# A recurrent attention kernel: the largest matrix product in row pairs of 64 rows, one pool of eight PSUM banks, and a searched scheduling bias

## The chip, the cores and the metric

The kernel runs on one core of a Trainium2 chip. The metric is the device time of one execution in microseconds (us), the median of several. A ratio is the mean time of one kernel's fast runs over that of the kernel before in the same rounds, so it is not quite the ratio of the medians that are quoted. Engines: PE is the matrix engine (PEld its weight loads), DVE is VectorE, ACT is ScalarE, POOL is GpSimd. PSUM is the memory of the tiles b, into which PE writes its sums (`b<-hT,Mw` in the profile). The granted clock is the mean share of its full clock that PE was allowed.

## The reference

Four residual layers in a row: attention, gated feed-forward, attention, feed-forward, each on the layer norm of x (2048 tokens of width 448). The attention layer has 16 heads of 256 and runs through 64 segments of 32 tokens, one after the other. Eight rows of memory go from each segment to the next, which makes the whole a recurrence:

```python
for s in range(n_seg):
    h = jnp.concatenate([mem, xs], axis=1)              # 8 + 32 rows
    q, k, v = h @ Wq, h @ Wk, h @ Wv                    # per head
    p = softmax(where(mask, q @ k.T * scale, -1e9))
    o = (p @ v) @ Wo
    mem = o[:, :M, :]
    outs.append(o[:, M:, :])
```

## The kernel before

The kernel multiplies the weights together once: M = Wq x Wk per head, N = Wv x Wo per head. A step is one segment of both attention layers (68 steps; the second layer runs four segments behind the first, and 60 steps have work for both layers, hence 80 columns). Its largest product is T = M x h: 56 blocks of 128 outputs (16 heads x 448 = 56 x 128), contraction 448, which the kernel pads to four tiles of 128 rows:

```python
def t_unit(self, t, c, u0, m):                 # m blocks into one PSUM bank
    R = S.tile("R", 1)
    def mms():
        b = R.b()
        return [MM(b[:, j*n:j*n + n], S.M[:, kt, 16*c + u0 + j, :],      # weights 128 x 128
                   S.hT[:, pp, s, kt, l0:l1, :].rearrange(...),         # moving 128 x n, n = 80
                   start=(kt == 0), stop=(kt == 3))
                for j in range(m) for kt in range(4)]
    S.mm(mms, 4 * m * S.pitch(n), rd, R.res() + dst)
    # ... then copies out of PSUM into TTm and TTs
```

That is 56 x 4 = 224 matmuls a step, each with a weight load of its own. A step goes on with the memory's scores (TTm x hT), a softmax, the product with h (PTm x hK), with N (Nw x UTm), the choice of the new memory rows (selm, and seln for a second layout), and the same for the segment (TTs x hT, PTs x hK, Nw x big); every second step also runs a feed-forward (xBT x big, hB x big).

The kernel divides PSUM into eight banks. A pool "R" hands out five of them; bank 4 is for the sums of Nw x big and of the feed-forward, banks 6 and 7 for the memory's chain:

```python
POOLS = {"R": [0, 1, 2, 3, 5]}
self.bO, self.bC = bank[4], bank[6:8]
# m_t writes b0 = bC[0]; m_nat, the seln product, writes the same b0
```

A scheduler orders all operations at build time with a small model of the engines. It keeps for each engine the time at which it comes free, counts a matmul of n columns as `max(25, n/2.4 + 2.6)` ns and a change of tile shape as 95 ns, and takes the ready operation with the longest path behind it:

```python
lim = max(f, t0) + (60.0 if e == "pe" else 40.0)
t, o = max((x for x in lst if x[0] <= lim), key=lambda x: (x[1].prio, -x[0]))
...
c = o.cost[e]
if e == "pe" and o.mode != mode:
    c += 95.0
    mode = o.mode
```

## Time and profile before

| | before |
|---|---|
| median, 3 runs | 1780.73 us (1775.98 to 1781.08) |
| span of the profiled execution | 1780.3 us |
| matmuls, each with a weight load | 30612 |
| granted clock of the matrix engine | 0.989 |

From the page of the kernel before, the busy times of the engines and, of its queues, the one that brings instructions (packets, MB, share of 16 engines):

```profile
PE 1700.7 (96%) x30612; PEld 1226.7 (69%) x30612; DVE 1073.2 (60%) x3058; ACT 720.6 (40%) x2031; POOL 91.0 (5%) x156
...
q8 instruction: 241, 3.95, 0.9%
```

PE is busy 96% of the span, so it is the bottleneck. Its busy time also counts the tails of pipelined matmuls (one of T takes 202 ns in the mean in the profile, and the next starts 36 ns after it), so a finer measure is wanted: the distance from the start of one matmul to the start of the next in the trace. Its median in this trace is 25 ns at 16 and at 40 columns, 36 ns at 80, 56 ns at 128 and 189 ns at 448. n/2.4 + 2.6 ns, with a floor of 25 ns, fits all of them; I call it the undisturbed *pitch*. The sum of the pitches of all matmuls is the *stream*, with concurrent tiles counted once, and all the rest of PE's time is *gaps*. The stream is thus a count of the work and not a measurement: it is the same for every kernel with the same matmuls, and time lost to a lower clock falls under gaps. Before: stream 1583 us, gaps 187 us.

The groups of instructions by form of the kernel before (count; busy us and mean ns; idle before them and what ended it):

```profile
L127 PE MATMUL b<-hT,Mw 128*128 128x80 bf16 x13440 | 496.5, 202 | 3.6 <-DVE hT L685 3.6
...
L127 PE MATMUL b<-hi,seln 128*128 128x448 bf16 x67 | 24.2, 360 | 14.9 <-ACT hT L684 14.9
```

The first line is T. The other is the seln product: it waits for ACT's copy into hT, since both use bank 6. Who made PE wait, longest total first (us in total, times, longest):

```profile
PE b L127 <- ACT hT L684: 14.9, 32, 0.5
PE b L127 <- DVE xn L721: 14.0, 21, 5.5
PE b L127 <- DVE XA L1008: 7.1, 14, 0.5
PE b L127 <- issue: 6.1, 6, 3.3
```

And one pass of T in the timeline (start, duration, both in us):

```profile
907.84 8.19 PE L127 MATMUL b<-hT,Mw 128*128 128x80 bf16 x224
```

That is 224 matmuls in 8.19 us including the tail of the last.

### The profile page before, as it was taken

What the parts mean: (1) busy time and instruction counts of PE and PEld (TensorE: products, weight loads), DVE (VectorE), ACT (ScalarE), POOL (GpSimd) and SP (SyncE); (2) the same over time, 40 slices, a digit from 0 to 9 for tenths busy, and PEclk for the clock granted to TensorE, in tenths of its full rate; (3) what the DMA queues carried; (4) which work ended last, traced back from release to release, by engine and by line L of the source; (5) the groups of instructions that cost most, each with busy time, mean ns of one, the idle gap of its engine ahead of it and who ended that gap; (6) DMA issues with size and microseconds to landing.
All of it is one profiled execution on the core that took longest, in us unless ns stands there. A gap on an engine that the chain in (4) does not pass through costs nothing.

```text
span 1780.3 us, 67770 instructions
## 1 busy us (share of the span) xinstructions
PE 1700.7 (96%) x30612; PEld 1226.7 (69%) x30612; DVE 1073.2 (60%) x3058; ACT 720.6 (40%) x2031; POOL 91.0 (5%) x156
## 2 busy tenths in 40 slices
PE   6899999999999999999999999999999999999997
PEld 2566766777677667767766776776677677667765
DVE  7647565565656556565655656565665656566554
ACT  5433433444443334444333444334344433434432
POOL 3000000000000000000000000000000000000000
PEclk9999999999999999999999999999999999999999
DMA  9700000000000000000000000000000000000000
GB/s 227 219 4 4 4 5 5 4 5 5 5 4 5 5 4 5 5 5 4 5 5 4 5 5 5 4 5 4 4 5 6 5 4 5 3 3 4 4 4 5
DMA packets 55760, 27.52 MB, mean 15 GB/s; under 512 B 44584, under 2 KB 54576, under 8 KB 55472
## 3 DMA queue, kind: packets, MB, share of 16 engines
q1 hardware_dynamic: 55120, 22.94, 5.3%
q8 instruction: 241, 3.95, 0.9%
q14 instruction: 47, 0.39, 0.1%
q10 hardware_dynamic: 352, 0.24, 0.1%
HBM read 10.33 MB, written 1.84 MB: 7 GB/s over the span
## 4 chain that ended last, share of the span: by engine, by line
PE 75%; DVE 6%; ACT 2%; issue 1%; DVEq 0%
PE b L127 75%; ACT big L684 1%; DVE big L685 1%; DVE stat L714 1%; DVE TTs L685 1%; DVE xn L721 1%; ACT hT L684 1%; DVE ys L1015 1%; DVE XA L1008 1%; DVE XB L968 0%; DVE Es L843 0%; DVE stat L842 0%; DVE TTm L685 0%; DVE hT L685 0%; DVE part L957 0%
## 5 line engine op out<-in xcount | busy, mean ns | idle before, releaser
L127 PEld LDWEIGHTS b<-hT,Mw 128*128 128x128 bf16 x15232 | 539.8, 100 | 25.3 <-DVE hT L685 11.2
L127 PE MATMUL b<-hT,Mw 128*128 128x80 bf16 (+1 forms) x15232 | 546.0, 200 | 5.0 <-DVE hT L685 4.6
L127 PE MATMUL b<-Nw,big 128*128 128x448 bf16 (+1 forms) x1936 | 394.9, 358 | 8.2 <-DVE big L685 5.6
L685 DVE CAST TTs<-b 128x320 bf16<-128x320 f32 (+5 forms) x574 | 261.3, 455 | 78.6 <-PE b L127 78.3
L127 PEld LDWEIGHTS b<-Nw,big 128*128 128x128 bf16 (+1 forms) x1936 | 163.7, 100 | 157.1 <-issue 21.5
L127 PE MATMUL b<-xBT,big 128*128 128x128 bf16 (+1 forms) x3808 | 219.6, 217 | 0.7 <-ACT xBT L684 0.7
L685 DVE CAST TTm<-b 128x80 bf16<-128x80 f32 (+5 forms) x580 | 134.7, 232 | 129.5 <-PE b L127 98.0
L127 PEld LDWEIGHTS b<-xBT,big 128*128 128x128 bf16 x3808 | 204.7, 98 | 2.4 <-ACT xBT L684 0.9
L127 PE MATMUL b<-Nw,UTm 128*32 128x448 bf16 x3752 | 192.0, 356 | 0.6 <-ACT UTm L684 0.6
L685 DVE CAST big<-b 128x512 bf16<-128x512 f32 (+1 forms) x190 | 121.3, 659 | 103.9 <-PE b L127 102.8
L684 ACT ACTIVATE big<-b 128x512 bf16<-128x512 f32 (+1 forms) x322 | 153.7, 525 | 48.2 <-PE b L127 45.0
L127 PEld LDWEIGHTS b<-Nw,UTm 128*32 128x32 bf16 x3752 | 95.2, 97 | 88.9 <-issue 18.7
L685 POOL COPY hK<-xn 32x448 bf16<-32x448 bf16 x136 | 75.6, 556 | 1521.6 <-DVE xn L721 1470.4
L684 ACT ACTIVATE TTs<-b 64x256 bf16<-64x256 f32 (+5 forms) x310 | 127.6, 412 | 29.6 <-PE b L127 22.4
L995 ACT ACTIVATE gT<-b 128x256 bf16<-128x256 f32 x226 | 86.4, 382 | 128.8 <-PE b L127 124.1
L684 ACT ACTIVATE TTm<-b 64x64 bf16<-64x64 f32 (+4 forms) x304 | 69.4, 228 | 159.4 <-PE b L127 152.5
L996 DVE TENSOR_TENSOR hB<-gT,b 128x256 bf16<-128x256 bf16 x226 | 93.6, 415 | 64.8 <-ACT gT L995 54.0
L896 ACT ACTIVATE hi<-b 128x448 bf16<-128x448 f32 x67 | 36.5, 544 | 193.7 <-PE b L127 193.5
L897 DVE TENSOR_TENSOR lo<-b,hi 128x448 bf16<-128x448 f32 x67 | 41.4, 619 | 121.2 <-ACT hi L896 121.2
L127 PE MATMUL b<-big,hB 128*128 128x448 bf16 (+1 forms) x476 | 107.3, 355 | 0.0
L684 ACT ACTIVATE hK<-b 8x448 bf16<-8x448 f32 x94 | 50.4, 536 | 122.5 <-PE b L127 121.0
L127 PE MATMUL b<-PTs,hK 40*128 40x512 bf16 (+1 forms) x640 | 86.4, 348 | 13.3 <-DVE XA L1008 7.1
(103 smaller groups left out, 1396.1 us busy)
## 6 DMA issues: line engine op xcount, KB each, us to landing
big<-in_A_Wo_dram SPq DMA_DIRECT2D x3, 896.0 KB, 5.8
out_dram<-ys SPq DMA_DIRECT2D x32, 56.0 KB, 1.9
big<-in_B_W_down_dram SPq DMA_DIRECT2D x1, 1568.0 KB, 6.8
XA<-in_A_x_dram SPq DMA_DIRECT2D x28, 56.0 KB, 2.0
big<-in_B_W_up_dram SPq DMA_DIRECT2D x1, 1344.0 KB, 8.1
big<-in_B_W_gate_dram SPq DMA_DIRECT2D x1, 1344.0 KB, 8.5
Nw<-in_A_Wo_dram SPq DMA_DIRECT2D x1, 896.0 KB, 6.4
XA<-in_A_x_dram ACTq DMA_DIRECT2D x4, 56.0 KB, 4.3
```

The source lines that it names most:

```text
L127: ins = E.matmul(out, lhsT=lhsT, rhs=rhs, **kw)
L684: return E.activation(out(), src(), ACT.Copy)
L685: return E.tensor_copy(out(), src())
L714: S.dve(lambda E: E.bn_stats(st[:, so:so + 6], x), D, rd, [(key, 0)])
L721: S.dve(lambda E, a=a, b=b, src=src: E.tensor_scalar(S.xn[:, i, a:b], src, st[:, so + 6:so + 7], st[:, so + 8:so + 9], op0=ALU.subtract, o ...
L896: S.act(lambda E: E.activation(S.hi[:, :], b[:, 0:D], ACT.Copy), D, S.ps(6), [("hi",)])
L897: S.dve(lambda E: E.tensor_tensor(S.lo[:, :], b[:, 0:D], S.hi[:, :], ALU.subtract), D, S.ps(6) + [("hi",)], [("lo",)])
L995: S.act(lambda E, k=k, R=R, n=n: E.activation(S.gT[:, k % 2, 0:n], R[0].b()[:, 0:n], ACT.Relu), n, R[0].res(), [("gT", k % 2)])
L996: S.dve(lambda E, k=k, R=R, n=n, fcs=fcs: E.tensor_tensor(S.hB[:, fcs[0]:fcs[-1] + 1, 0:w], S.gT[:, k % 2, 0:n].rearrange("p (a b) -> p a ...
L1008: S.dve(lambda E: E.tensor_tensor(S.XA[64:128, q % 4, :], S.bO[0:64, 0:D], S.XB[0:64, p % 2, :], ALU.add), D, S.ps(4, half=(0,)) + xb, [(" ...
L1015: S.dve(lambda E: E.tensor_tensor(S.ys[64:128, p % 2, :], S.bO[64:128, 0:D], S.XB[64:128, p % 2, :], ALU.add), D, S.ps(4, half=(1,)) + xb, ...
```

## The change

The intent is to take the padding out of T. A product with only 64 rows leaves the other 64 of 128 free, and two such products on different row halves can run at once: in the trace before, the two matmuls of a row pair of PTm x hK start 3 to 4 ns apart, and pairs of 128 columns follow each other after 56 ns, the pitch of a single 128-column matmul (the first pair after a change of tile shape takes 67 ns). T is cut into pieces of 64 rows (448 = 7 x 64), and two blocks A and B go side by side: first A on the upper half of the rows and B on the lower, then exchanged. A slot is the time of one matmul, or of two that run at once. A pair of blocks takes 14 matmuls in 7 slots; the 28 pairs of a step take 392 matmuls in 196 slots, where 224 slots were used before. In this kernel the two halves write to different banks, and the second half of a group waits for its first. All eight banks go into one pool, and each kind of work gets a bias on its priority, found by an offline search that minimises the span in the scheduler's own engine model. The core of the diff (the rest renames fixed banks to pool tiles):

```diff
+BIAS = {
+    "b_down": -20822.0, "b_layer": 11731.0, "ln_a": 5000.0, "ln_b": 8278.0, "m_nat": -8730.0, "m_t": 19893.0,
+    "p_t_mem": 13944.0, "s_mem": 20000.0, "s_seg": 38611.0, "seg_pt": 10000.0, "t_pass": 80290.0, "u_mem":
+    -2223.0, "u_seg": -245.0, "un": -6353.0, "un_mem": -500.0,
+}
...
-    POOLS = {"R": [0, 1, 2, 3, 5]}
+    POOLS = {"R": list(range(8))}
...
+        for o in self.ops:
+            o.prio += BIAS.get(o.cat, 0.0)
...
-        self.M = self.sb("Mw", [128, 4, NO, 128])
+        self.M = self.sb("Mw", [128, 3, NO, 128])
+        self.M3 = self.sb("M3", [128, NO // 2, 128])
...
+                    if not second:
+                        for kt in range(3):
+                            out.append(MM(a[:, v], S.M[top, kt, oa + j, :], mov(kt, top), start=(j == kt == 0), stop=False))
+                            out.append(MM(b[:, v], S.M[bot, kt, ob + j, :], mov(kt, bot), start=(j == kt == 0), stop=False))
+                        out.append(MM(a[:, v], S.M3[top, slot0 + j, :], mov(3, top), start=False, stop=False))
+                        out.append(MM(b[:, v], S.M3[bot, slot0 + j, :], mov(3, bot), start=False, stop=False))
+                    else:
+                        for kt in range(3):
+                            e = j == m - 1 and kt == 2
+                            out.append(MM(b[:, v], S.M[top, kt, ob + j, :], mov(kt, top), start=False, stop=e))
+                            out.append(MM(a[:, v], S.M[bot, kt, oa + j, :], mov(kt, bot), start=False, stop=e))
...
+            S.mm(mms, (3 if second else 4) * m * S.pitch(n), rd + rd2 if second else rd, ..., mode=1)
```

The last line tells the model that a pair costs one pitch: 4 or 3 slots a block pair, each 36 ns.

## The prediction

> **What bounds the kernel now.** The matrix engine. The page's first part has PE busy 1700.7 of 1780.3 us, VectorE 60%, ScalarE 40%; DMA is idle after two of 40 slices; PE is at 9 tenths nearly throughout, at full clock. I split PE time by the matmuls' start-to-start distances in the trace. They follow n/2.4 + 2.6 ns with a floor of 25 ns: 36 ns at 80 columns, 56 at 128, 189 at 448. With concurrent tiles counted once, these pitches sum to about 1583 us. The other 187 us are gaps: about 74 us in 721 changes of tile shape (95 to 125 ns each), 40 us of start-up, 70 us of steady waits. The largest: the seln matmul waiting for ScalarE's hT copy, as both use one fixed bank (18 us), PTs x hK waiting for VectorE (14 us), the first Nw x big waiting for the copy into big (12 us).

> **What changes.**
> 1. T (Mw x hT) was 224 matmuls per step, contraction padded from 448 to 512 rows: 8.05 us per step, 528 us in all. It becomes 392 matmuls of 64 rows, two at once on different row halves and banks: 196 slots. If a pair costs one pitch: 28 slots x 36 ns x 60 two-layer steps + 28 x 25 ns x 8 others = **-66 us**. Row pairs already in the trace (PTm x hK, 40x128) start 3 ns apart, and pairs follow each other after 56 ns, as one 128-column matmul would; the first pair after a shape change loses 11 ns, as a single full load does, so two loads run together. [...] Not shown: four instructions per 36 ns sustained for 7 us; the trace sustains two per 25 ns.
> 2. Shape changes: 697 instead of 721 by the order listing: -2 us.
> 3. Eight banks in one pool, no fixed banks: removes the 18 us wait and part of the others. I credit **-20 us** net, bias included.
> 4. Costs: T's copies still take VectorE and ScalarE about 9 us of work per step; the new order wants the segment scores (TTs x hT) about 1 us after T, when copies may still run (0.1 to 0.4 us per step). 32 more setup copies, at most 3 us. PE's wait for its own first half is covered by 0.5 us or more of another pair.

> **On the path.** PE is the bottleneck, so removed stream time counts fully while the recurrence (about 18.6 us in the timeline) stays under the step period (26 us, then about 25).

> **Prediction: 1692 us**, range 1655 to 1740. Chances: faster by over 2% 0.88, within 2% 0.07, slower 0.05.

> **What would show each step.** (1) T's stretch in the timeline 7.0 to 7.2 us for 392 matmuls, pairs 36 ns apart. (2) 95 to 125 ns before and after T. (3) No ScalarE hT wait before hi x seln; PE idle down from about 80 to about 60 us. (4) Idle before TTs x hT released by VectorE or ScalarE.

> **What would make it wrong.** If pairs are limited by instruction issue or loads (50 ns a pair), T takes 9.8 us and the kernel gets slower than before. If copies or banks stall the pairs inside T, gain shrinks towards 1740. If the search removes most steady waits, about 1660.

The sum: 1780 - 66 - 2 - 20 = 1692 us.

## The result

| | before | changed |
|---|---|---|
| median, 4 runs each | 1780.9 us | 1877.3 us (1876.34 to 1885.94) |
| ratio of fast runs | | 1.0552 (95%: 1.051 to 1.0594) |
| matmuls | 30612 | 42036 |
| changes of tile shape on PE | 721 | 697 |
| stream (pitches of all matmuls) | 1583 us | 1517 us |
| gaps | 187 us | 347 us |
| granted clock of the profiled execution | 0.989 | 0.974 |
| pass of T, first to last matmul start, median of 60 | 8.11 us | 9.41 us (shortest 8.68) |

The change is slower by 5.5%, where 5% faster was predicted. The stream is smaller by the 66 us that the prediction gave it; as it is counted with the same pitches, that is arithmetic. What the trace confirms is the pitch: one pair of T starts 36 ns after the other (median), as one 80-column matmul does. The gaps grew by 160 us. From the page of the changed kernel, the same two lines:

```profile
PE 1663.3 (89%) x42036; PEld 1185.6 (63%) x42036; DVE 974.5 (52%) x2797; ACT 805.8 (43%) x2459; POOL 88.0 (5%) x155
...
q8 instruction: 332, 5.44, 1.2%
```

PE is busy for less time, in a longer span; it idles more. The instruction queue brought 332 packets instead of 241. The same groups of instructions ("hT,M" is the new array M3, its number left out):

```profile
L131 PE MATMUL b<-hT,Mw 64*128 64x80 bf16 x20160 | 454.7, 198 | 105.5 <-issue 103.6 <-PE b L131 1.0 <-DVE hT L699 0.6
...
L131 PE MATMUL b<-hT,M 64*128 64x80 bf16 x3360 | 264.8, 198 | 18.0 <-issue 18.0
...
L131 PE MATMUL b<-hi,seln 128*128 128x448 bf16 x67 | 23.6, 352 | 0.0
```

The seln product waits for nothing now, as predicted. But the two groups of T stand 124 us idle, nearly all of it "issue": time in which the engine waited for nothing that the profile shows. Who made PE wait:

```profile
PE b L131 <- issue: 167.5, 161, 4.8
PE b L131 <- DVE xn L735: 23.0, 32, 6.2
...
PE b L131 <- PE b L131: 1.0, 1, 1.0
```

"PE b <- PE b" would be the wait for the first half: 1.0 us in all. So in this profile neither banks nor copies nor the first half hold T up. The timeline in one pass of T shows where the idle time lies:

```profile
906.44 0.20 PE L131 MATMUL b<-hT,M 64*128 64x80 bf16 x2
906.48 0.23 PE L131 MATMUL b<-hT,Mw 64*128 64x80 bf16 x3
907.63 0.24 PE L131 MATMUL b<-hT,Mw 64*128 64x80 bf16 x3 [0.92 <-issue]
907.68 0.24 PE L131 MATMUL b<-hT,M 64*128 64x80 bf16 x2
...
909.37 0.23 PE L131 MATMUL b<-hT,M 64*128 64x80 bf16 x2
909.40 0.70 PE L131 MATMUL b<-hT,Mw 64*128 64x80 bf16 x28
911.51 0.41 PE L131 MATMUL b<-hT,Mw 64*128 64x80 bf16 x8 [1.41 <-issue]
...
913.04 0.74 PE L131 MATMUL b<-Nw,big 128*128 128x448 bf16 x3
```

Between two stalls T runs at its full pace (64 pairs in 2.3 us, 36 ns a pair); the stalls fall at odd places, in the middle of a group. Counting instructions explains the places. In program order, a matmul is two instructions (load and product, 42036 of each in the trace), anything else one (871 here). The changed kernel has 84943 instructions for PE, 331.8 blocks of 256; the instruction queue brought 332 packets, each of 16384 bytes, 64 for each of 256 instructions. The kernel before has 61792, 241.4 blocks, and its queue brought 241 packets. In the trace 145 of the 146 stalls of over 0.15 us inside T begin at position 193 to 197 of a block of 256, together 183 us. The other stall is 0.5 us. The queue itself, in the DMA view of this pass cut into 40 slices of 0.26 us (GB/s, then packets, MB and share):

```profile
GB/s 0 0 0 0 0 0 0 62 0 0 0 0 0 0 0 0 0 0 0 0 0 62 0 0 0 0 0 0 0 0 0 0 0 0 0 0 0 62 0 0
...
q8 instruction: 3, 0.05, 2.2%
```

Three refills in the pass, one for each block that T uses up, near 904.9, 908.8 and 912.8 us. Over the whole trace a refill starts a median of 2.5 us before the stall that it ends (162 cases), and the next refill starts only after the engine has entered the new block: 1.2 us after the end of the stall in the median of the 146, 1.06 us at the soonest. Where two stalls end in successive blocks, 3.75 us lie between them (median of 94 cases, shortest 3.35). A block of T's row pairs is used up in 2.3 us. A block of the old T took 4.6 us (128 matmuls x 36 ns), longer than those 3.75 us, and it shows no such stalls (one in the whole trace).

One rival has to be set aside first: the granted clock fell from 0.989 to 0.974. The clock of both kernels in 40 slices of the span, in tenths of full speed, before and changed:

```profile
PEclk9999999999999999999999999999999999999999
PEclk9879999999999999999999999999999999999878
```

The lower clock lies at the start and the end. From 200 to 1700 us it is 1.00 in both traces, and 118 of the 146 stalls, 137 us, begin there. PE ran at half clock (128-column matmuls 107 ns apart instead of 56) for 98 us in all, against 40 us before; at most half of the other 58 us is lost by it, an estimate that leaves most of the 160 us to something else.

### The profile page after: what moved, and what is told of

Read it like the earlier page. It is cut to its first block, busy times and chain, and to the rows that moved or that the text cites. A ratio compares the mean times of both kernels' runs of the same rounds, so it can differ in the third digit from the quotient of the medians.

```text
span 1874.5 us, 91186 instructions
## 1 busy us (share of the span) xinstructions
PE 1663.3 (89%) x42036; PEld 1185.6 (63%) x42036; DVE 974.5 (52%) x2797; ACT 805.8 (43%) x2459; POOL 88.0 (5%) x155
## 5 line engine op out<-in xcount | busy, mean ns | idle before, releaser
L131 PE MATMUL b<-hT,Mw 64*128 64x80 bf16 (+1 forms) x22848 | 503.3, 196 | 134.2 <-issue 131.9
L131 PEld LDWEIGHTS b<-hT,Mw 64*128 64x128 bf16 x22848 | 479.2, 97 | 167.0 <-issue 149.8
L131 PE MATMUL b<-Nw,big 128*128 128x448 bf16 (+1 forms) x1936 | 412.4, 357 | 1.4 <-issue 1.4
L131 PE MATMUL b<-hT,M 64*128 64x80 bf16 (+1 forms) x3808 | 293.4, 196 | 24.7 <-issue 24.7
L699 DVE CAST TTm<-b 128x80 bf16<-128x80 f32 (+6 forms) x448 | 97.9, 226 | 388.0 <-PE b L131 387.1
L698 ACT ACTIVATE TTm<-b 128x80 bf16<-128x80 f32 (+6 forms) x504 | 106.5, 224 | 388.9 <-PE b L131 388.2
L131 PEld LDWEIGHTS b<-hT,M 64*128 64x128 bf16 x3808 | 202.9, 97 | 25.7 <-issue 25.7
L699 DVE CAST TTs<-b 128x320 bf16<-128x320 f32 (+5 forms) x476 | 200.6, 432 | 5.9 <-PE b L131 5.9
L698 ACT ACTIVATE TTs<-b 128x320 bf16<-128x320 f32 (+5 forms) x476 | 180.1, 396 | 6.6 <-PE b L131 6.6
L698 ACT ACTIVATE big<-b 128x512 bf16<-128x512 f32 x317 | 159.7, 566 | 5.4 <-PE b L131 3.8
```

Of the source, the lines that this page charges most:

```text
L131: ins = E.matmul(out, lhsT=lhsT, rhs=rhs, **kw)
L698: return E.activation(out(), src(), ACT.Copy)
L699: return E.tensor_copy(out(), src())
```

## The experiments

The table collects the accounting of all versions of the whole kernel, worked out from each trace as above, the granted clock of the profiled execution among it; "block end" is the sum of stalls over 0.15 us inside T at positions 192 to 198 of 256. Medians are of 4 runs, in each case beside runs of the kernel before on the same chip.

| run | T | banks, bias | median us | ratio | stream | gaps | shape changes | block end in T | granted clock |
|---|---|---|---|---|---|---|---|---|---|
| before | full | fixed, none | 1780.9 | 1 | 1583 | 187 | 721 | 0.5 | 0.989 |
| changed | pairs | pool, searched | 1877.3 | 1.055 | 1517 | 347 | 697 | 182.8 | 0.974 |
| e1_full | full | pool, same | 1903.2 | 1.069 | 1583 | 307 | 608 | 3.2 | 0.958 |
| e3_nobias | pairs | pool, none | 1956.4 | 1.100 | 1517 | 436 | 1167 | 76.0 | 0.937 |
| e5_hybrid | last 64 rows paired | pool, same | 1715.7 | 0.964 | 1517 | 186 | 940 | 7.0 | 0.991 |
| e7_pairs_only | pairs | fixed, none | 2115.1 | 1.187 | 1517 | 584 | 1324 | 21.3 | 0.953 |
| e8_full_nobias | full | pool, none | 1766.3 | 0.991 | 1583 | 172 | 677 | 1.9 | 0.990 |
| e9_hybrid_nobias | last 64 rows paired | pool, none | 1809.8 | 1.016 | 1517 | 281 | 1033 | 1.7 | 0.953 |
| e10_hybrid_re | last 64 rows paired | pool, searched again | 1685.2 | 0.947 | 1517 | 153 | 908 | 2.3 | 0.994 |
| e11_refill | pairs | pool, searched with a refill rule | 1824.6 | 1.022 | 1517 | 299 | 887 | 85.5 | 0.988 |

All of them gave correct results. In e1, e3, e7 and e9 the granted clock is lower through the whole span: their traces show PE at half clock for 163, 248, 200 and 172 us, in many short stretches, against 23 to 98 us in the others. In e9 one 80-column matmul starts 67 ns after the other there, and 36 ns elsewhere. In the stretches of e1 and e9 that were looked at, the half clock comes just after a wait of PE (3.0 us in e1, 1.4 us in e9); no run tests what starts it.

### e6_probe: the disputed cost by itself

Four runs of 1024 matmuls were added at the end of the kernel before, on PE alone:

```diff
+            for s, v in ends:              # ACT, DVE and POOL have finished
+                E.wait_ge(s, v)
+            def full(n, count):
+                for i in range(count):
+                    E.matmul(S.banks[0][:, 0:n], lhsT=S.M[:, i % 3, i % NO, :], rhs=mv[:, 0:n], start=True, stop=True)
+            def pairs(n, count):
+                for i in range(count // 2):
+                    for h, b in ((slice(0, 64), 1), (slice(64, 128), 2)):
+                        E.matmul(S.banks[b][:, 0:n], lhsT=S.M[h, i % 3, i % NO, :], rhs=mv[h, 0:n], start=True, stop=True)
+            full(80, 1024); pairs(80, 1024); full(16, 1024); pairs(192, 1024)
```

> The kernel before, with four runs of 1024 matmuls each (2048 instructions, eight blocks of 256) added at its end, on the matrix engine alone, with nothing to wait for and results unused: full array 80 columns, row pairs 80 columns, full array 16 columns, row pairs 192 columns. F: pairs of 80 columns take 27 to 31 us instead of 18.4 us, with a stall of over 1 us at most block ends; the 16 columns, at 25 ns a matmul 25.6 us if unlimited, take 27 to 31 us too though they are no pairs; full 80 columns take 36 to 38 us and pairs of 192 columns 42 to 44 us, with no stalls. D: pairs of 80 columns take 18 to 20 us, for there is no bank, copy or half to wait for. A theory that row pairs as such stall (banks or rows colliding): pairs of 192 columns stall too, and 16 full columns don't.

Measured, start of the first to start of the last: 36.65, 27.45, 29.43 and 44.57 us (one run; the clock at the pairs of 80 columns was 1.00). The timeline of the probe's stretch:

```profile
1779.87 36.85 PE L506 MATMUL b<-hT,Mw 128*128 128x80 bf16 x1024 [1.43 <-issue]
1816.66 3.36 PE L511 MATMUL b<-hT,Mw 64*128 64x80 bf16 x177
1821.01 2.47 PE L511 MATMUL b<-hT,Mw 64*128 64x80 bf16 x128 [0.99 <-issue]
1824.49 2.47 PE L511 MATMUL b<-hT,Mw 64*128 64x80 bf16 x128 [1.01 <-issue]
1827.96 2.47 PE L511 MATMUL b<-hT,Mw 64*128 64x80 bf16 x128 [1.01 <-issue]
...
1844.23 1.38 PE L506 MATMUL b<-hT,Mw 128*128 128x16 bf16 x49
1846.44 7.05 PE L506 MATMUL b<-hT,Mw 128*128 128x16 bf16 x256 [0.82 <-issue]
1853.66 3.58 PE L506 MATMUL b<-hT,Mw 128*128 128x16 bf16 x128 [0.16 <-issue]
...
1861.15 12.69 PE L506 MATMUL b<-hT,Mw 128*128 128x16 bf16 x463 [0.17 <-issue]
1873.77 44.81 PE L511 MATMUL b<-hT,Mw 64*128 64x192 bf16 x1024
```

With nothing to wait for, pairs of 80 columns stop after every 128 matmuls, that is every 256 instructions, for 1.0 to 1.6 us. Blocks last 3.46 to 4.02 us instead of the 2.3 us that the same pairs take without the stall. Only the first full block of pairs, which follows slow ones, passes in 2.3 us; the first stop comes 177 matmuls (354 instructions) after the pairs began. Pairs of 192 columns, whose blocks last 5.28 us, never stop. So row pairs as such run freely; it is the number of instructions in a time that is limited. That rules out theory D for these stalls. The full array with 16 columns is less clean: it also stopped at block ends, though it has no pairs, but for 0.16 us most times, and the mean granted clock was 0.57 in this stretch, and a matmul took 26.7 ns rather than 25. It agrees with F, but does not carry it. The total of the last run passed the expected 44 us by 0.6; the clock was 0.94 there.

### e5_hybrid: the same slots with fewer instructions

Only the odd 64 rows of the contraction need pairing. The other 384 rows are three full tiles:

```diff
-        part(g, R[g], False) ... part(g, R[g], True)      # 392 matmuls of 64 rows
+    PLAN = [("full", (0, 1)), ("rows", (0, 1, 2)), ("full", (2, 3)), ("rows", (3, 4, 5)), ("full", (4, 5))]
+        # full(g): kt = 0, 1, 2 of both units of pair g on the full array, 128 rows
+        for j in range(m):
+            for kt in range(3):
+                out.append(MM(T.b()[:, j*n:j*n + n], S.M[:, kt, 16*c + u0 + j, :], S.hT[:, pp, s, kt, l0:l1, :], ...))
+        # rows(gs): the last 64 rows, unit A on the upper half, unit B on the lower
+        for j in range(m):
+            out.append(MM(R[g][0].b()[:, v], S.M3[top, slot0 + j, :], mov(3, top), start=st, stop=e))
+            out.append(MM(R[g][1].b()[:, v], S.M3[bot, slot0 + j, :], mov(3, bot), start=st, stop=e))
```

That is 168 + 56 = 224 matmuls in 168 + 28 = 196 slots. The pool, the bias and the rest are the changed kernel's.

> The changed kernel with only the last 64 rows of T's contraction in row pairs (56 matmuls in 28 slots, in two bursts), the other 384 rows in 168 full matmuls: the same 196 slots as the change, with 448 instructions a step instead of 784, and four changes of tile shape a step inside T. F: a block of 256 instructions lasts about 4.0 us in T, longer than the 3.75 us refill, so stalls at block ends nearly vanish (under 0.3 us a step); T takes 7.3 to 7.9 us with its shape changes; time 1680 to 1740 us. D: banks are held as long as in the change or longer and copies start later, so the stalls inside T stay (over 1 us a step), time over 1780 us.

Measured: 1715.73 us, ratio 0.9638 (95%: 0.9621 to 0.9656), T in 7.71 us (median). The two lines of its page:

```profile
PE 1648.6 (96%) x30612; PEld 1173.3 (68%) x30612; DVE 998.0 (58%) x2909; ACT 778.5 (45%) x2347; POOL 87.7 (5%) x155
...
q8 instruction: 242, 3.96, 0.9%
```

The instructions are back at 242 packets, PE is busy 96% again, and the stalls at block ends inside T fell from 183 to 7 us, 0.1 us a step. T holds no fewer banks at once (six during a burst) and its copies are the same, so waits for banks or copies don't explain the 183 us either. The cost that the split brings is also in the table: 243 more changes of tile shape than the changed kernel. Inside T, where nothing else is waited for, one costs 98 ns (median of 272), about 24 us in all, an estimate from these two numbers. This version beats both kernels.

### e1_full, e3_nobias, e8_full_nobias, e9_hybrid_nobias: what the bias and the pool do

e1 puts the old T into the changed kernel (`t_pass` calls `t_unit` above for each unit; M has four tiles again); e3 sets `BIAS = {}`; e8 does both; e9 is e5 with `BIAS = {}`.

> The changed kernel with T put back on the full array (224 matmuls of 128 rows a step); eight banks in one pool and the bias kept. Theory F (the matrix engine's instruction stream is refilled in blocks of 256 instructions; a refill takes about 3.75 us when T's row pairs use one up in 2.3 us): the stalls at one fixed place in every block of 256 disappear, the steps' stream grows back by 66 us to about 1583 us, and the time is 1695 to 1755 us, with 5.6 us or less lost inside all T passes. Theory B (the searched bias made a worse order): still at or above 1800 us. Theory D (the pairs wait for banks, copies or their own first half): also fast, so this run does not tell F from D.

> The changed kernel with every bias set to nothing; row pairs and the pool of eight banks kept. F: T still stalls about twice a step for 1.1 us at the same place of each block of 256 instructions (100 us or more in all, unless other work happens to be placed inside T); time 1830 to 1930 us. B: time at or under 1780 us and the stalls inside T gone.

> The changed kernel with T on the full array and no bias: the kernel before with the pool of eight banks alone. It tells why the full array with the searched bias took 1903 us. If the bias, searched for another T, is what hurts there: 1740 to 1800 us. If the pool of eight banks hurts by itself: 1830 us or more. F expects no stalls at the block ends in either case.

> The version with only the last 64 rows paired, without the bias. F: no stalls at block ends; the time tells what the bias is worth to a T that does not stall. If the bias is worth about what it was between the two versions with full pairs (1956 against 1877 us, 79 us): 1760 to 1830 us.

e1 missed its time: 1903.2 us, not 1695 to 1755. Its stalls at block ends are gone as F said (3 us), but other waits came. Who made its PE wait:

```profile
PE b L131 <- DVE xn L735: 57.3, 33, 5.1
PE b L131 <- DVE Pm L830: 43.9, 16, 3.0
PE b L131 <- issue: 7.3, 4, 3.3
```

The new waits are for DVE's layer norm (xn) and the memory's softmax (Pm), not for instructions. e8 shows why: the same kernel without the bias takes 1766.28 us (ratio 0.9908, 95%: 0.9881 to 0.9936). So the bias, searched for the model's idea of row pairs, costs an old T 137 us (1903.2 - 1766.3; up to 63 us of it can be the clock, half of the 163 - 36 us more at half clock), and the pool of eight banks alone is worth 0.9%. e3 took 1956.38 us, above the 1830 to 1930 expected, with 76 us of stalls at block ends rather than 100 or more; I put that down to other work between T's parts (1167 changes of tile shape), which stretches the blocks. So here the bias helps by 79 us, although it packs T tightly and more than doubles the stalls (76 to 183 us). For the hybrid it helps by 94 us (1809.8 to 1715.7), within the 1760 to 1830 us that was expected of e9. Both gains go together with the clock, which is lower without the bias (0.937 against 0.974, and 0.953 against 0.991), so how much of them is a better order alone is not shown. Theory B falls as the cause of the loss: taking the bias away from the changed kernel makes it slower. But the bias is worth what it is worth only together with the T that it was searched for.

### e7_pairs_only: row pairs in the kernel before

The changed `t_pass`, `t_copies`, M3 and the wait for the first half were put into the kernel before, with its fixed banks and no bias.

> The kernel before with T in row pairs alone: fixed banks, pool of five, no bias. The order listing shows 1324 changes of tile shape against 721, because without the bias the scheduler puts other work between T's parts; at about 100 ns each that costs 60 us. F: stream -66 us, shape changes +60 us, and stalls at the same place in the blocks of 256 instructions, fewer than in the change because other work inside T stretches the blocks (0.5 to 2 per step, 40 to 140 us): 1810 to 1930 us. If the pool or the bias were the cause instead of the pairs, this one shows no such stalls and takes 1760 to 1790 us.

Measured: 2115.08 us, ratio 1.187, far outside the expected range. The stalls at block ends inside T are only 21 us; other stalls came in their place: 125 further gaps of 119 us inside T. Who made its PE wait:

```profile
PE b L131 <- DVE TTs L689: 133.3, 181, 1.2
PE b L131 <- DVE Es L893: 54.1, 28, 1.9
```

With five banks in the pool, T waits for DVE to copy TTs out. Here theory D's mechanism is real and I had not reckoned with it: T has four banks in work and two more being copied, which five banks can't serve, and without the bias the order is poor besides. The parts of the change can't be added up one by one.

### e10_hybrid_re: the bias searched again

The same search idea (random steps on the biases, keeping what shortens the scheduler's own span, 840 seconds) was run for the hybrid:

```diff
-BIAS = { ... the changed kernel's ... }
+BIAS = {"b_down": -22829, "b_layer": 26760, "ln_a": 86029, "ln_b": 75302, "m_nat": -12510, "m_t": 203841, "p_t_mem": 529037,
+        "s_mem": 23429, "s_seg": 17526, "seg_pt": -6015, "t_pass": 127155, "u_mem": -5686, "u_seg": -2501, "un": -14682, "un_mem": 210608}
```

> The version with only the last 64 rows paired, its bias searched again with the kernel's own engine model for this T (840 seconds of a random search; the same shape of T, 908 changes of tile shape instead of 940). If the model is sound wherever blocks of instructions last over 3.75 us: faster than the 1716 us of the bias taken over, 1675 to 1710 us, with no more stalls at block ends (under 0.3 us a step).

Measured: 1685.23 us, ratio 0.9469 (95%: 0.9434 to 0.9504), the fastest of all. Its page, its waits, and one pass of T in the timeline:

```profile
PE 1634.2 (97%) x30612; PEld 1172.0 (70%) x30612; DVE 992.4 (59%) x2856; ACT 803.1 (48%) x2400; POOL 87.7 (5%) x155
...
q8 instruction: 242, 3.96, 1.0%
```

```profile
PE b L131 <- DVE xn L731: 22.0, 33, 6.2
PE b L131 <- issue: 6.1, 4, 2.5
```

```profile
905.77 2.31 PE L131 MATMUL b<-hT,Mw 128*128 128x80 bf16 x60
908.02 0.71 PE L131 MATMUL b<-hT,M 64*128 64x80 bf16 x30
908.66 1.25 PE L131 MATMUL b<-hT,Mw 128*128 128x80 bf16 x30
909.74 0.54 PE L131 MATMUL b<-Nw,big 128*128 128x448 bf16 x2
910.12 1.24 PE L131 MATMUL b<-hT,Mw 128*128 128x80 bf16 x30
911.29 0.64 PE L131 MATMUL b<-hT,M 64*128 64x80 bf16 x26
911.87 1.82 PE L131 MATMUL b<-hT,Mw 128*128 128x80 bf16 x46
```

"issue" is 6 us in the whole span. T's bursts of row pairs (30 and 26 matmuls, 60 and 52 instructions) are too short to use up a block. Nothing in the model was changed for this run; the one run agrees with a model that is good enough where blocks last long enough.

### e11_refill: all pairs, with a refill rule in the model

```diff
+    BLOCK, REFILL = 256, 3600.0
+            if e == "pe":
+                o.count = 8 if o.mode == 5 else 2 * len(o.fn())
+                left, at, step = o.count, t, c / o.count
+                while left:
+                    k = min(left, self.BLOCK - issued)
+                    at, left, issued = at + k * step, left - k, issued + k
+                    if issued == self.BLOCK:
+                        issued, at = 0, max(at, entered + self.REFILL)
+                        entered = at
+                c = at - t
```

> The changed kernel with all of T in row pairs; the scheduler's engine model gets one more rule (a block of 256 instructions of the matrix engine lasts at least 3.6 us, from the 3.47 us of the probe and the 3.75 us median of the change), a bias of its own for each of T's twelve parts, and the bias is searched again for 30 minutes under that rule. F: by letting other work in between T's parts the search can win back part of the stalls, but not make 784 instructions fit in 7 us: 1790 to 1850 us, faster than the change's 1877 us, slower than the version with 448 instructions (1685 us); stalls at the block ends 60 to 130 us in all. If the refill were not the cause, a search that models it would gain nothing: 1870 us or more.

Measured: 1824.57 us, ratio 1.0219 (95%: 1.0202 to 1.0236), inside the range. The longest of its waits:

```profile
PE b L131 <- issue: 86.6, 98, 2.9
```

It won back 53 us of the changed kernel's loss (1877.3 - 1824.6), in which the stalls at block ends inside T went from 183 to 86 us. The run changed three things at once (the rule, a bias for each of T's parts, a new search), so the 53 us are not the rule's alone; the fewer stalls are what it was to bring. Such a search can spread T, but the kernel stays slower than the kernel before: 784 instructions are three blocks, over 11 us at 3.75 us each, in a pass that has 7 us of stream.

## Why the prediction was wrong

- **"If a pair costs one pitch ... -66 us"**: the pitch held. Pairs follow each other after 36 ns wherever they run, and the counted stream fell from 1583 to 1517 us. The two matmuls of a pair of T start 3 ns apart in the median (3 to 4 ns in the trace before, in 180 pairs of PTm x hK).
- **The step that failed** stands at the end of the same point: "Not shown: four instructions per 36 ns sustained for 7 us; the trace sustains two per 25 ns." It was listed as a risk, costed at 50 ns a pair, and then given a weight of 0 in the sum and of 0.05 in the chances. The missing term measured 183 us. The mechanism named there ("instruction issue or loads") was wrong in kind as well: it is no slower pitch of each pair but a stop at the end of a block, 1.2 us in the median (half of them between 0.9 and 1.6 us). That T's 9.41 us lies near the 9.8 us named for this risk is a coincidence. The trace before could have warned: 241 instruction packets of 16384 bytes are in it, and a block of the old T lasted 4.6 us. It held only a few blocks shorter than 3.4 us (the shortest 3.17), so it could not give the limit itself.
- **"Removed stream time counts fully while the recurrence stays under the step period"** failed with it. PE was the bottleneck, but what bound it inside T was not the array.
- **"-20 us net" for banks and bias**: agrees, but only by subtraction. The gaps outside these stalls are 347 - 183 = 164 us against 187, and the wait of seln went from 14.9 us to 0.0. Without the 183 us the changed kernel would stand at 1694 us, by subtraction, next to the 1692 predicted; that is arithmetic, not a run. e5 and e10 are the runs: 1716 and 1685 us with the same stream.
- **Shape changes**: 697 by the trace as by the listing; 98 ns each inside T in e5, and 96 ns in the median of the 721 in the trace before (90 to 117 ns where no wait adds to it), much as in "95 to 125 ns".
- **"If copies or banks stall the pairs inside T"**: not in the changed kernel (one other stall, 0.5 us), but in e7 with five banks (119 us).

What stays open: why a block's refill takes about 3.5 us from entering the block before (of that, 1.2 us pass before it starts, and 1.07 us are the packet's own time in the queue; medians of the changed kernel), and why some loops of the probe took 4.0 us. Also left open in part is why the hybrid without bias (1810 us) is slower than the full T without bias (1766 us), though its stream is 66 us smaller. The table and the traces account for most of the 109 us by which its gaps are larger: 356 more changes of tile shape, about 35 us at 98 ns each, and 136 us more at half clock, of which up to 68 us are lost. Both are estimates; what starts the half clock is not known.

## What to carry to other kernels

Count instructions as well as slots: in these traces a matmul with its load is two, and before cutting matmuls into smaller ones that run side by side, divide the time of 256 instructions by what the runs show a block to need (here 3.35 us at the shortest and 3.75 us in the median of the changed kernel, 3.46 to 4.02 us in the probe; 3.75 us is about 15 ns an instruction). Pair only the part that saves slots: the odd 64 rows gave the whole saving of 28 slots with the old number of instructions. A search over a model optimises what the model counts; check its first winner on the chip for a term that it lacks, and search again when a part of the kernel changes, for the bias that gained 94 us with one T cost 137 us with another.
